# Gate product on VectorE from PSUM, every second unit's spectral products on GpSimd: a recurrence with a long convolution on one Trainium2 core

## Chip, cores and metric

The kernel runs on one core of a Trainium2 chip. The metric is device time in microseconds for one launch, the median over runs. The five instruction queues named below are TensorE (PE, with its weight loads as PEld), VectorE (DVE), ScalarE (ACT), GpSimd (POOL) and SyncE (SP, which issues the DMAs).

## What is computed

For each of 4 batches of 6272 steps and 256 channels, all float32 at the interface:

```python
sig = 1 / (1 + exp(-f_logit))
f = lower_bound + (1 - lower_bound) * sig
for t in range(6272):                       # a gated recurrence, per channel
    h = f[:, t] * h + (1 - f[:, t]) * x[:, t]
    y[:, t] = h
x1, x2, x3 = split(y @ w_proj, 3)           # 256 channels each
conv = irfft(rfft(x2) * rfft(filter_fft))   # circular, 6272 long, per channel
out = (x1 * conv * x3) @ w_out
```

## The kernel before

**Numbers of the transform.** 6272 is 128 times 49, so the long transform is two short ones written as matrix products: one over 128 points, one over 49. Channels are taken in pairs, 128 pairs in all, and handled in 16 *units* of 8 pairs.

**Stages of one batch.**
- *Recurrence* (`hgrn`): 13 pieces of 512 steps. `x` and `f_logit` are loaded, ScalarE makes the sigmoid (`sig`, L392), GpSimd multiplies it into x (`u`, L394, tile `XT`), TensorE transposes both (`sT`, `uT`, L401), ScalarE or VectorE makes the gate (`f`, L415), VectorE scans (`scan`, L423) into the f16 tile `HA`. GpSimd copies a part of the result behind its end (`wrap`, L371).
- *P*: the projection for x2, 98 matmuls (L730), copied out by ScalarE or VectorE (`x2`, into `X2`).
- *Spectrum*, per unit: first transform (`F1`, L743), its copy `A`, second transform (`F2`, L788) into two PSUM banks; two products with the filter's spectrum (`prod`, L801, on VectorE, 98 partitions by 1008) into tile `PP`; a small sum for frequency zero (`slot`, L793, on GpSimd), then the first inverse transform (`I2`, L811), and its copy `Th`. Every fourth unit has a `mini` product for frequency zero (L759, L765). The filter's spectrum was made in the setup, lies in DRAM and is fetched unit by unit into `Hu`. `PP` has two buffers (`NP = 2`), so even units use buffer 0 and odd units buffer 1; `Hu` has three.
- *Gate* (`gate`): in 13 column pieces of 490 and for two channel halves, 26 pieces a batch, two matmul pairs make x1 and x3 (`x13`, L450, one PSUM bank each); ScalarE copies both to SBUF (`xs`, L462, tiles `x1s` and `x3s`, two buffers); GpSimd multiplies them and writes the product regrouped from steps to the transform's order, f16, into `zt` (`z`, L466).
- *Output* (`phase_o`), 13 groups: the second inverse (`I1`, L844), VectorE multiplies it with `zt` (`y`, L850), TensorE applies w_out (L862), ScalarE or VectorE copies out (`o`, L363 on ScalarE), SyncE stores. The first `y` needs every `z` and, through I1, every `Th` of its batch; `zt` has one buffer, so the next batch's `z` follow this batch's last `y`.

A setup of about 88 us makes the transform tables and the filter's spectrum, beside batch 0's recurrence.

**What sets the order.** Nothing is issued as written. Each piece of work is an `op` with a guessed cost on each engine that may run it, and the class `Plan` simulates the engines and the 8 PSUM banks and picks the next op by earliest start, an urgency (longest way to the end, plus tables `LEAD` and `TILT` by kind and batch) and a shyness by kind and engine (`SHY`). Ops with several engines in their cost (the PSUM copies, `f`, `wrap`) go to the one it picks. It then emits every engine's queue in that order. PSUM is one tile of 8 banks, a matmul op takes one or two of them (`take`) and the last op that reads them frees them. So a change of one op's engine, cost or weight can move the whole order, the setup's too. The lines of the gate before:

```python
op("xs", {"ACT": 0.05 + n / 1200.0}, ...)          # for x1 and for x3
op("z", {"POOL": 0.1 + 3.68 * n / 1000}, ...,
   r=[("x1s", j, 0), ("x1s", j, 1), "cv"], w=[("z", jb, c)])
```

Of the kernel before, what the change touches and what calls it, by code (L numbers as in the profile page):

```python
# [9 lines left out]
F32 = mybir.dt.float32  # L10
# [3 lines left out]
AOP = mybir.AluOpType  # L14
AF = mybir.ActivationFunctionType
# [9 lines left out]
Q = 49  # L25
TB = 98
CH = 512
# [13 lines left out]
ZS = 64.0  # L41
# [16 lines left out]
class Plan:  # L58
# [11 lines left out]
    FROM = {"PE": 0.0, "ACT": 0.0, "DVE": 0.8, "POOL": 0.8, "SP": 0.75}  # L70
    TURN = 0.097
    COLD = 7.5
    SHY = {("A", "ACT"): 27, ("A", "DVE"): 27, ("Th", "ACT"): -10, ("Th", "DVE"): 779,
            ("afs", "ACT"): 51, ("afs", "DVE"): -12, ("f", "ACT"): -4, ("f", "DVE"): 452,
            ("f2", "ACT"): 100, ("f2", "DVE"): 126, ("fr", "ACT"): 290, ("fr", "DVE"): 2705,
            ("fr", "POOL"): -84, ("hw", "ACT"): -32, ("hw", "DVE"): 364, ("o", "ACT"): 13,
            ("o", "DVE"): 1968, ("wrap", "ACT"): 1376, ("wrap", "POOL"): 115, ("x2", "ACT"): 90,
            ("x2", "DVE"): 63}

    STICK = 4.0  # L80
    ROWS = ("F2", "mini", "I1", "FF2", "last")
    LANES = 8

    TILT = {
        "A": (10, -421, 208, -185), "F1": (-87, -1, 1, -163), "F2": (297, -97, -22, -362),
        "FF1": (-72, 0, 0, 0), "FF2": (-79, 0, 0, 0), "H": (-184, 334, 22, 133),
        "I1": (-280, -65, -92, 13), "I2": (-282, -43, -206, 0), "P": (-10, -2, 64, -49),
        "Th": (-3, -372, 21, -100), "afs": (-31, 0, 0, 0), "f": (-348, -382, -7, -601),
        "f2": (206, 0, 0, 0), "ff": (-455, 0, 0, 0), "fr": (-21, 0, 0, 0), "hst": (-91, 0, 0, 0),
        "hw": (11, 0, 0, 0), "load": (-7, -238, -192, 0), "mX": (18, 0, 0, 0),  # L90
        "mini": (-412, 357, -19, 94), "o": (0, -19, 214, 0), "pad": (14, 0, 0, 0),
        "prod": (0, -199, -22, 1135), "proj": (387, -1338, -11, 254), "rot": (-287, 0, 0, 0),
        "sT": (-25, 1516, -37, 149), "scan": (-40, -6, -71, -138), "sig": (-116, 262, -46, -451),
        "slot": (-6, -10, -78, 18), "store": (-23, -498, 174, 242), "tabs": (335, 0, 0, 0),
        "u": (-6, 0, -48, 383), "uT": (-1369, -27, 23, 104), "warm": (-427, 0, 0, 0),
        "wrap": (0, 312, 253, 2), "x13": (-140, -373, -471, -159), "x2": (35, -288, 339, 160),
        "xs": (2160, 1264, 0, 301), "y": (-27, 470, 49, -42), "z": (0, 0, 532, 756),
        "zm": (1130, 0, -12, 65),
    }

    LEAD = {
        "A": (35, -373, 1648, 137), "F1": (462, -629, 1502, 4000), "F2": (5639, 140, 319, 1412),
        "FF2": (-1269, 0, 0, 0), "H": (0, -477, -796, -1751), "I1": (-67, 978, 15, 184),
        "I2": (-35, -8, 4207, 55), "P": (-34, -342, 3292, -57), "Th": (164, 540, 125, 0),
        "args": (598, 0, 0, 0), "f": (294, -69, -69, -264), "f2": (-491, 0, 0, 0),
        "ff": (5684, 0, 0, 0), "fr": (505, 0, 0, 0), "hst": (566, 0, 0, 0), "hw": (-475, 0, 0, 0),
        "iden": (346, 0, 0, 0), "iota": (33, 0, 0, 0), "last": (43, 0, 0, 0),
        "load": (1910, -587, 70, -424), "mX": (103, 0, 0, 0), "mini": (162, -443, 3560, 2034),
        "o": (182, 252, -11, 418), "pad": (-134, 0, 0, 0), "pre": (-656, 0, 0, 0),
        "prod": (53, -700, 0, 7), "proj": (-7749, -9436, -6234, 114), "rest": (109, 0, 0, 0),  # L110
        "sT": (0, -96, -2, -1), "scan": (-892, 17, -1191, -2973), "sig": (0, 79, 43, 146),
        "slot": (126, 219, 502, 1379), "store": (-387, -299, -79, -369), "tabs": (5294, 0, 0, 0),
        "turns": (-46, 0, 0, 0), "u": (801, 3, 107, 648), "uT": (10, -692, -6798, -121),
        "warm": (-40, 0, 0, 0), "wcol": (443, 0, 0, 0), "wl": (-474, 0, 0, 0),
        "wrap": (-936, -549, -39, 333), "x13": (-350, -2412, -46, -1943), "x2": (0, 0, 1048, 2601),
        "xs": (5528, -104, 106, -88), "y": (-100, -570, -30, -285), "z": (-742, -2, 69, 0),
        "zm": (236, 148, 847, -6),
    }

    def __init__(self):  # L120
# [157 lines left out]
def kernel(  # L278
# [10 lines left out]
    nc = tc.nc  # L289
# [4 lines left out]
    op = plan.op  # L294

    konst = ctx.enter_context(tc.tile_pool(name="konst", bufs=1))
    iden = konst.tile([128, 128], F32, name="iden")
# [9 lines left out]
    W13 = konst.tile([128, 2, 512], F16, name="W13")  # L307
# [19 lines left out]
    Hu = konst.tile([128, NH, 2, 2, UE * 64], F16, name="Hu")  # L327
# [45 lines left out]
    def either(n, runs=1.0):  # L373

        return {"ACT": 0.045 + runs * n / 1200.0, "DVE": 0.07 + n / 960.0}
# [61 lines left out]
    def gate(b):  # L437
        for c in range(NCHK):
            m0 = c * XR
            nm = min(XR, 128 - m0)  # L440
            hn = [("hn", kh, i) for kh in range(2) for i in range(max(c - 1, 0), c + 1)]
            t0, n = m0 * Q, nm * Q
            for jb in range(2):
                x13 = []
                for i in range(2):
                    js = slice(i * 256 + jb * 128, i * 256 + jb * 128 + 128)

                    def mm(e, p, js=js, t0=t0, n=n):
                        for kh in range(2):
                            nc.tensor.matmul(PS[:, p, 0:n], W13[:, kh, js],  # L450
                                             HA[:, HB[kh] + t0:HB[kh] + t0 + n],
                                             start=(kh == 0), stop=(kh == 1))
                    x13.append(op("x13", {"PE": 0.005 + 2 * n / 2400.0}, mm,
                                  r=hn + ["W13"], w=["qX"], take=1))
                j = count["s"] % 2
                count["s"] += 1

                def xs(i, j=j, n=n):
                    return late["x3s" if i else "x1s"][:, j, 0:n]
                for i in range(2):  # L460
                    op("xs", {"ACT": 0.05 + n / 1200.0}, lambda e, p, xs=xs, n=n, i=i:
                       nc.scalar.activation(  # L462
                           xs(i), PS[:, p, 0:n], AF.Copy, scale=1.0 if i else ZS),
                       r=["cv"], w=[("x1s", j, i)], src=x13[i])
                op("z", {"POOL": 0.1 + 3.68 * n / 1000}, lambda e, xs=xs, jb=jb, m0=m0, nm=nm:
                   nc.gpsimd.tensor_tensor(  # L466
                       late["zt"][:, jb, :, m0:m0 + nm],
                       xs(0).rearrange("p (m r) -> p r m", r=Q),
                       xs(1).rearrange("p (m r) -> p r m", r=Q), op=AOP.mult),
                   r=[("x1s", j, 0), ("x1s", j, 1), "cv"], w=[("z", jb, c)])  # L470


    def prepare(tmp):
# [300 lines left out]
    def unit(b, u):  # L774
# [7 lines left out]
        def mm(e, xb):  # L782
# [11 lines left out]
            PP[:TB, k, :, :, :, 0], zp[:TB, u // NA % 2, :, :, 0, ka:ka + UE],  # L794
            zp[:TB, u // NA % 2, :, :, 1, ka:ka + UE], op=AOP.add),
           r=[("zp", u // NA % 2), "D1"], w=[("Pz", k, 0), ("Pz", k, 1)])
        for o in range(2):
            def prod(e, xb, o=o):
                px = PS[:TB, xb + o, :].rearrange("p (i k) -> p i k", k=64)[:, :, 1:64]
                hh = Hu[:TB, h, :, o].rearrange("p a (i k) -> p a i k", k=64)  # L800
                nc.vector.tensor_tensor(  # L801
                    PP[:TB, k, o, :, :, 1:64],
                    px.unsqueeze(1).broadcast_to([TB, 2, UE, 63]), hh[:, :, :, 1:64],
                    op=AOP.mult)
            op("prod", {"DVE": 1.11}, prod, r=[("Hu", h)], w=[("P", k, o)], src=f2, part=o)

        def inv(e, ib):
            for o in range(2):
# [68 lines left out]
    with tc.manual_schedule():  # L877
        scope = ctx.enter_context(ExitStack())
        prepare(scope.enter_context(tc.tile_pool(name="tmp", bufs=1)))
        hgrn(0)  # L880

        def turn(e):

            scope.close()
            cv = ctx.enter_context(tc.tile_pool(name="cv", bufs=1))

            late["zt"] = cv.tile([128, 2, Q, 128], F16, name="zt")
            late["Th"] = cv.tile([128, TB, 2, 64], F16, name="Th")
            late["ys"] = cv.tile([128, 2, 2, 512], F32R, name="ys")
            late["x1s"] = cv.tile([128, 2, CH], F32, name="x1s")  # L890
            late["x3s"] = cv.tile([128, 2, CH], F32, name="x3s")
            late["osb"] = [cv.tile([128, 4, 256], F32, name=f"osb{i}") for i in range(NO)]
        op("pre", {"SP": 0.01}, turn, r=FF1 + FF2, w=["cv"])

        for b in range(B):
            plan.batch = b
            spectrum(b)
            gate(b)
            phase_o(b)
            if b + 1 < B:  # L900
                plan.batch = b + 1
                hgrn(b + 1)
        plan.emit()
# [30 lines left out]
```

## Time and profile before

| | |
|---|---|
| median of 11 runs | 507.8 us (505.46 to 510.57) |
| the profiled execution | 508.18 us, its span 506.4 us |
| granted TensorE clock, mean | 0.994 |
| instructions | 13245 |
| DMA traffic | 116.39 MB, mean 230 GB/s |

The span runs from the first to the last instruction of the program on the chip; the time has 1.8 us more around it. Times in the profile are microseconds unless marked ns. A group of instructions reads: line, engine, operation, out<-in by the program's tile names, shapes, count, then busy time, mean ns of one, and the engine's idle time just before, with what ended it. The busy time of TensorE has modelled ends, since its matmuls are pipelined.

### The profile page before, as it was taken

To read this page: it belongs to the slowest core of one execution; us is meant where nothing else is said; L and a number is where in the kernel's file an instruction comes from. 1 tells how busy PE (TensorE), PEld (TensorE's weight loads), DVE (VectorE), ACT (ScalarE), POOL (GpSimd) and SP (SyncE) were. 2 spreads that over 40 slices of the span, in tenths; PEclk is the share of its full clock that TensorE was granted. 3 is DMA by queue.
4 is the path that set the end of the run, shared out by engine and by line. 5 is a ranking of instruction groups with operands and counts; after the bars stand their busy time and mean duration, and the time that the engine had idled before them with its cause. 6 is when DMAs were issued, how large, how long until landed. Compare 5 with 4: busy or idle time off the path is not lost. (4 is left out here: it accounts for less than half of the span.)

```text
span 506.4 us, 13245 instructions
## 1 busy us (share of the span) xinstructions
PE 479.4 (95%) x5257; PEld 373.9 (74%) x5257; DVE 444.0 (88%) x451; ACT 410.8 (81%) x587; POOL 386.5 (76%) x328
## 2 busy tenths in 40 slices
PE   8979998999999999998998999999999999999795
PEld 6767775866777899766766889666778887566584
DVE  8789996888999999888996999899999978989763
ACT  3658868999998787898898788899988767999554
POOL 8886765899999845599799848889989633998700
PEclk9999999999999999999999999999999999999999
DMA  8979999536678998256668997166798870345156
GB/s 333 408 231 291 322 299 300 193 109 187 211 217 270 299 354 305 97 180 172 206 208 282 294 328 318 42 191 179 245 297 287 308 287 12 97 132 158 34 237 273
DMA packets 41725, 116.39 MB, mean 230 GB/s; under 512 B 4384, under 2 KB 6304, under 8 KB 41664
## 3 DMA queue, kind: packets, MB, share of 16 engines
q1 hardware_dynamic: 41664, 115.56, 68.1%
q8 instruction: 41, 0.67, 0.6%
q14 instruction: 20, 0.16, 0.1%
HBM read 84.54 MB, written 31.00 MB: 228 GB/s over the span
## 5 line engine op out<-in xcount | busy, mean ns | idle before, releaser
L466 POOL TENSOR_TENSOR zt<-x1s,x3s 128x490 f16<-128x490 f32 (+1 forms) x104 | 201.5, 1953 | 39.7 <-ACT x3s L462 19.3
L801 DVE TENSOR_TENSOR PP<-PS,Hu 98x1008 f16<-98x1008 f32 x128 | 146.7, 1198 | 11.4 <-ACT x1s L462 3.9
L394 POOL TENSOR_TENSOR XT<-XT,FL 128x1024 f32<-128x1024 f32 (+1 forms) x52 | 117.2, 2257 | 36.8 <-DMA XT<-in_x_dram 18.2
L423 DVE TENSOR_TENSOR_SCAN HA<-fTs,HA,PS 128x512 f16<-128x512 f32 (+1 forms) x96 | 113.9, 1203 | 10.6 <-PE PS L401 7.4
L450 PE MATMUL PS<-HA,W 128*128 128x490 f16 (+1 forms) x416 | 106.3, 367 | 1.5 <-DVE PP L801 1.0
L415 ACT ACTIVATE fTs<-PS,nomc 128x512 f32<-128x512 f32 (+1 forms) x104 | 69.4, 669 | 20.3 <-PE PS L401 13.1
L850 DVE TENSOR_TENSOR ys<-PS,zt 128x1024 fp32r<-128x1024 f32 (+1 forms) x52 | 59.9, 1159 | 15.0 <-PE PS L844 8.3
L363 ACT ACTIVATE osb<-PS 128x1024 f32<-128x1024 f32 (+1 forms) x52 | 50.7, 978 | 22.0 <-PE PS L862 19.9
L401 PE MATMUL PS<-iden,XT 128*128 128x128 f32 x392 | 62.5, 280 | 3.7 <-ACT fTs L415 1.6
L462 ACT ACTIVATE x1s<-PS 128x490 f32<-128x490 f32 (+1 forms) x104 | 60.9, 585 | 5.7 <-PE PS L450 3.7
L862 PE MATMUL PS<-Wo,ys 128*128 128x256 f32 x392 | 60.3, 296 | 3.5 <-DVE ys L850 2.0
L462 ACT ACTIVATE x3s<-PS 128x490 f32<-128x490 f32 (+1 forms) x104 | 60.6, 584 | 3.3 <-POOL zt L466 2.1
L401 PE MATMUL PS<-iden,FL 128*128 128x128 f32 x392 | 60.6, 275 | 0.3 <-ACT FL L392 0.3
L392 ACT ACTIVATE FL<-FL 128x1024 f32<-128x1024 f32 (+1 forms) x52 | 52.6, 1015 | 7.8 <-DMA FL<-in_f_logit_dram 7.7
L811 PEld LDWEIGHTS <-PP 98*128 98x128 f16 x1024 | 50.1, 98 | 10.8 <-issue 2.6
L862 PEld LDWEIGHTS PS<-Wo,ys 128*128 128x128 f32 x392 | 50.5, 192 | 8.0 <-DVE ys L850 2.7
L361 ACT CAST Th<-PS 128x784 f16<-128x784 f32 x64 | 52.7, 824 | 4.2 <-PE PS L811 3.7
L401 PEld LDWEIGHTS PS<-iden,XT 128*128 128x128 f32 x392 | 44.1, 140 | 16.1 <-POOL XT L394 2.6
L450 PEld LDWEIGHTS <-W 128*128 128x128 f16 x416 | 34.7, 97 | 27.0 <-issue 8.7
L811 PE MATMUL PS<-VA,PP 98*128 98x98 f16 x512 | 52.4, 207 | 1.5 <-DVE PP L801 0.7
L811 PE MATMUL PS<-VB,PP 98*128 98x98 f16 x512 | 52.1, 207 | 0.0
L366 DVE CAST X<-PS 128x1024 f16<-128x1024 f32 (+1 forms) x34 | 46.9, 1481 | 5.2 <-PE PS L730 3.9
(98 smaller groups left out, 700.4 us busy)
## 6 DMA issues: line engine op xcount, KB each, us to landing
Hu<-H SPq DMA_DIRECT2D x64, 392.0 KB
FL<-in_f_logit_dram SPq DMA_DIRECT2D x48, 512.0 KB
XT<-in_x_dram SPq DMA_DIRECT2D x48, 512.0 KB
out_dram<-osb SPq DMA_DIRECT2D x48, 512.0 KB
X<-in_moe_filter_fft_dram SPq DMA_DIRECT2D x9, 512.0 KB
H<-Hu SPq DMA_DIRECT2D x16, 196.0 KB
H<-Hu SPq DMA_DIRECT2D x16, 128.0 KB
Hu<-in_moe_filter_fft_dram SPq DMA_DIRECT2D x2, 512.0 KB
```

The lines of the kernel that those rows point to most:

```text
L361: nc.scalar.copy(dst, src)
L394: op("u", {"POOL": 0.1 + 0.553 * nb}, lambda e, xt=xt, ft=ft: nc.gpsimd.tensor_tensor(xt, xt, ft, op=AOP.mult), r=[("ft", k)], w=[("xt", k)])
L401: nc.tensor.transpose(PS[:, p, j:128 * nb:nb], src[:, j, cols], iden[:])
L415: nc.scalar.activation(fT, PS[:, p, 0:n], AF.Identity, scale=by, bias=1.0)
L423: nc.vector.tensor_tensor_scan(h, fT, PS[:, p, 0:n], init, op0=AOP.mult, op1=AOP.add),
L450: nc.tensor.matmul(PS[:, p, 0:n], W13[:, kh, js], HA[:, HB[kh] + t0:HB[kh] + t0 + n], start=(kh == 0), stop=(kh == 1))
L462: nc.scalar.activation(xs(i), PS[:, p, 0:n], AF.Copy, scale=1.0 if i else ZS),
L466: nc.gpsimd.tensor_tensor(late["zt"][:, jb, :, m0:m0 + nm], xs(0).rearrange("p (m r) -> p r m", r=Q), xs(1).rearrange("p (m r) -> p r m", ...
L801: nc.vector.tensor_tensor(PP[:TB, k, o, :, :, 1:64], px.unsqueeze(1).broadcast_to([TB, 2, UE, 63]), hh[:, :, :, 1:64], op=AOP.mult)
L811: nc.tensor.matmul(PS[:, ib + o, pr * TB:(pr + 1) * TB], PP[:TB, k, o, n, 2 * pr:2 * pr + 2, :], v[:TB], start=(n == 0), stop=(n == 1))
L850: nc.vector.tensor_tensor(late["ys"][:, yk, :, 0:rn * 128], PS[:, cb:cb + 2, 0:rn * 128], late["zt"][:].rearrange("p k r m -> p k (r m)") ...
L862: nc.tensor.matmul(po[:, i, :], late["ys"][:, yk, kh, i * 128:(i + 1) * 128], Wo[:, kh, :], start=(kh == 0), stop=(kh == 1))
```

## The change

The copy of x1 to SBUF goes. x3 is made first and copied by ScalarE with the scale that x1 had; VectorE then multiplies x1, straight from its PSUM bank, with it, and writes `zt`. For odd units the two banks of F2 are copied to a new SBUF tile `Xc` (one buffer, in the space of `x1s`) by ScalarE or VectorE, and GpSimd makes both products from it (`prodp`). Even units keep theirs on VectorE. The tables `SHY`, `TILT` and `LEAD` have other values throughout; the new kinds `xc` and `prodp` are in them. Costs of all other ops, buffer counts and the matmuls are as they were.

```diff
     SHY = {("A", "ACT"): 31, ("A", "DVE"): 44, ...,
+           ("xc", "ACT"): 24, ("xc", "DVE"): 452}
 ...
-                x13 = []
-                for i in range(2):
+                x13 = {}
+                for i in (1, 0):
 ...
-                for i in range(2):
-                    op("xs", {"ACT": 0.05 + n / 1200.0}, lambda e, p, xs=xs, n=n, i=i:
-                       nc.scalar.activation(
-                           xs(i), PS[:, p, 0:n], AF.Copy, scale=1.0 if i else ZS),
-                       r=["cv"], w=[("x1s", j, i)], src=x13[i])
-                op("z", {"POOL": 0.1 + 3.68 * n / 1000}, lambda e, xs=xs, jb=jb, m0=m0, nm=nm:
-                   nc.gpsimd.tensor_tensor(
+                op("xs", {"ACT": 0.05 + n / 1200.0}, lambda e, p, j=j, n=n: nc.scalar.activation(
+                    late["x3s"][:, j, 0:n], PS[:, p, 0:n], AF.Copy, scale=ZS),
+                   r=["cv"], w=[("x3s", j)], src=x13[1])
+                op("z", {"DVE": 0.1 + n / 930.0}, lambda e, p, j=j, n=n, jb=jb, m0=m0, nm=nm:
+                   nc.vector.tensor_tensor(
                        late["zt"][:, jb, :, m0:m0 + nm],
-                       xs(0).rearrange("p (m r) -> p r m", r=Q),
-                       xs(1).rearrange("p (m r) -> p r m", r=Q), op=AOP.mult),
-                   r=[("x1s", j, 0), ("x1s", j, 1), "cv"], w=[("z", jb, c)])
+                       PS[:, p, 0:n].rearrange("p (m r) -> p r m", r=Q),
+                       late["x3s"][:, j, 0:n].rearrange("p (m r) -> p r m", r=Q), op=AOP.mult),
+                   r=[("x3s", j), "cv"], w=[("z", jb, c)], src=x13[0])
 ...
+        beside = u % 2 == 1
+        if beside:
+            op("xc", either(1024), lambda e, xb: copy(e, late["Xc"][:TB], PS[:TB, xb:xb + 2, :]),
+               r=["cv"], w=["Xc"], src=f2)
         for o in range(2):
-            def prod(e, xb, o=o):
-                px = PS[:TB, xb + o, :].rearrange(...)[:, :, 1:64]
+            def prod(e, xb=None, o=o):
+                px = (late["Xc"][:TB, o] if beside else PS[:TB, xb + o, :]).rearrange(...)[:, :, 1:64]
                 hh = Hu[:TB, h, :, o].rearrange("p a (i k) -> p a i k", k=64)
-                nc.vector.tensor_tensor(
+                (nc.gpsimd if beside else nc.vector).tensor_tensor(
                     PP[:TB, k, o, :, :, 1:64],
                     px.unsqueeze(1).broadcast_to([TB, 2, UE, 63]), hh[:, :, :, 1:64],
                     op=AOP.mult)
-            op("prod", {"DVE": 1.11}, prod, r=[("Hu", h)], w=[("P", k, o)], src=f2, part=o)
+            if beside:
+                op("prodp", {"POOL": 2.4}, prod, r=[("Hu", h), "Xc"], w=[("P", k, o)])
+            else:
+                op("prod", {"DVE": 1.11}, prod, r=[("Hu", h)], w=[("P", k, o)], src=f2, part=o)
 ...
-            late["x1s"] = cv.tile([128, 2, CH], F32, name="x1s")
+            late["Xc"] = cv.tile([128, 2, 512], F32, name="Xc")
```

## Prediction

> **What bounds the kernel now.** I read the page first: five engines close together.
>
> ```profile
> PE 479.4 (95%) x5257; PEld 373.9 (74%) x5257; DVE 444.0 (88%) x451; ACT 410.8 (81%) x587; POOL 386.5 (76%) x328
> ```
>
> TensorE is busiest, but a whole-span share hides stages, so I cut the span by stage (a batch's spectrum, then its inverse and output with the next recurrence). Columns: stretch, length, busy time (instructions) of PE, PEld, DVE, ACT, POOL, clock, DMA share, GB/s.
>
> ```profile
> 104.40:160.00 55.60, 54.81 (x647) 39.29 (x647) 52.62 (x53) 53.03 (x86) 53.55 (x41) 1.00 0.66 209
> 210.00:265.00 55.00, 52.77 (x627) 36.78 (x623) 51.65 (x52) 48.60 (x79) 49.56 (x41) 1.00 0.60 182
> 317.20:366.90 49.70, 49.42 (x600) 34.61 (x599) 46.14 (x47) 46.62 (x74) 45.89 (x38) 1.00 0.55 166
> 423.50:466.00 42.50, 41.82 (x513) 27.37 (x512) 38.16 (x38) 38.82 (x62) 37.53 (x30) 1.00 0.36 108
> 466.00:479.80 13.80, 10.80 (x158) 7.00 (x156) 10.47 (x12) 9.39 (x17) 11.60 (x10) 1.00 0.23 61
> ```
>
> In the spectrum stages VectorE, ScalarE and GpSimd all run at 88 to 96% beside a full TensorE; none is spare. The durations come from the groups by line:
>
> ```profile
> L466 POOL TENSOR_TENSOR zt<-x1s,x3s 128x490 f16<-128x490 f32 x96 | 188.8, 1982 | 39.0 <-ACT x3s L462 19.3 <-DVE ys L850 12.6 <-DMA XT<-in_x_dram 4.1
> L801 DVE TENSOR_TENSOR PP<-PS,Hu 98x1008 f16<-98x1008 f32 x128 | 146.7, 1198 | 11.4 <-ACT x1s L462 3.9 <-ACT x3s L462 3.3 <-ACT Th L361 1.8
> L394 POOL TENSOR_TENSOR XT<-XT,FL 128x1024 f32<-128x1024 f32 x48 | 114.3, 2383 | 35.5 <-DMA XT<-in_x_dram 16.9 <-ACT FL L392 11.0 <-ACT fTs L415 7.4
> L466 POOL TENSOR_TENSOR zt<-x1s,x3s 128x392 f16<-128x392 f32 x8 | 12.8, 1610 | 0.7 <-ACT x1s L462 0.7
> L394 POOL TENSOR_TENSOR XT<-XT,FL 128x256 f32<-128x256 f32 x4 | 2.9, 736 | 1.3 <-DMA XT<-in_x_dram 1.3
> L850 DVE TENSOR_TENSOR ys<-PS,zt 128x1024 fp32r<-128x1024 f32 x48 | 58.1, 1217 | 14.9 <-PE PS L844 8.3 <-POOL zt L466 3.3 <-ACT osb L363 1.8
> L850 DVE TENSOR_TENSOR ys<-PS,zt 128x256 fp32r<-128x256 f32 x4 | 1.9, 464 | 0.1
> ```
>
> Last, the chain that ended last, at the turn from spectrum to output of batch 3 (start, length, what):
>
> ```profile
> 466.85 1.55 POOL zt L466
> 468.77 0.55 POOL PP L793 x2
> 469.32 0.98 POOL zt L466
> 470.30 0.79 issue
> 471.45 1.81 POOL zt L466
> 473.56 3.36 POOL zt L466 x2
> 476.92 1.54 POOLq L929
> 478.48 1.24 DVE ys L850
> ```
>
> The last z ends at 478.4 and the first y starts. But the timeline has that batch's last spectral inverse (L811) ending at 476.4 and its first output inverse (L844) at 477.3: z and spectrum finish together, so removing z there buys at most 1 us. In batches 1 and 2 L811 ends at 266.9 and 375.1 and y starts at 276.4 and 383.4, each right after the last z (276.0, 383.4): 9.5 and 8.3 us, against 2.9 and 2.1 in batches 0 and 3. TensorE filled that time with the next batch's transposes (17.18 of 17.8 us from 366.9 to 384.7), so most of it isn't lost.
>
> **TensorE's floor.** Pieces of the same chain view: F1 8 matmuls 0.45 to 0.55 us, F2 0.54, I2 0.70, four gate matmuls 0.83, four transposes 0.44, 16 of L844 0.56, 8 of L862 0.95, and 98 of L730 in 10.8. Per batch: 16x(0.5+0.54+0.70) + 26x0.83 + 98x0.22 + 12.25x(0.56+0.95) + 10.8 = 100 us. The batches' L730 starts (88.5, 193.7, 306.2, 413.7) are 105, 112.5 and 107.5 apart; the last batch takes 87.4 against 78 without transposes. So some 34 us at most is there to win.
>
> **The change part by part.**
> *VectorE.* It loses 64 of 128 products: 64x1.198 = 76.7 us. It gains 104 z from PSUM. By y's two sizes, (1217-464)/768 = 0.98 ns an element over 0.21 us: 0.69 for 490, 0.60 for 392, in all 71 us. z reads at a stride of 49 and writes runs of 10 f16. The filter's copy reads PSUM as far apart at 692 ns for 512 (against 677 for a plain 512), so a strided read needn't cost; the X copies that write runs of four f16 take 1501 for 1024, 1.47 ns, which makes z 0.93 and the sum 96. I take 0.69, as the runs are longer: -5 us net, +20 at worst; below nothing is excluded, since both operands are f32.
> *ScalarE.* It loses 104 x1 copies, 60.9 us, and gains 32 copies of 1024 from PSUM, 1.02 us each by the A copy (46.9/46): 33 us. Net -28. On VectorE each would be 1.21.
> *GpSimd.* It loses all z, 201.5 us. It gains 64 products of 1008. Near end: the x-times-gate product has packed operands, (2383-736)/768 = 2.14 ns, so 2.35 us. Far end: z's slope (1982-1610)/98 = 3.8 ns, 3.95 us; low end a one-input f32 copy, 1.05 us for 1024. The new operands are packed in runs of 63, so I take 2.35: 150 us, net -51. That GpSimd is slowed by VectorE's work beside it does not show: the gate products took 2.35 to 2.47 us whichever VectorE rows ran at the time.
> GPSIMD Engine Reference in the Trainium skill (Performance pitfalls) says reads with a step over 8 bytes cost half as much again; the two slopes, 3.8 at a 196-byte step against 2.14, agree in sign and show more. By the page's ratio a packed product would be 3.8/1.5 = 2.5 ns an element, 2.7 us (an estimate), and my sum 6 us higher. Against the change, the same page (Engine selection) tells one to keep two-input elementwise work on VectorE, GpSimd being about twice as slow; it gives 4497 ns for 2048, by which (an estimate) a product is 2.21 us and my sum 2 us lower (16 products of batch 3's chain).
>
> *Where that sits.* All three feeders get lighter, VectorE and ScalarE by 33 us together. The flexible copies (A, X, filter) can be spread over both, and over batches 0 to 2 the two spare 25 us, 12.6 each, 13.7 of time at 92% occupancy if they set the pace throughout. TensorE's floor takes part back: I count two thirds, -9. Of the 6 us each that y waited for z in batches 1 and 2, a quarter, -3, as TensorE was filled.
>
> *What is added to a chain.* Product tile PP has two buffers by unit parity and the new Xc one, so GpSimd's next unit starts only after I2 read the last product, and after the copy that waits for the last product to leave Xc. A pair of units costs GpSimd 2x2.35 for products, 0.4 for two slot sums (0.2 from start to start by the timeline), and idle time: a hand-over (0.08, from x3's copy at 466.77 to z), 1.02 of copy, another, perhaps 0.3 behind other work on a 91% busy ScalarE, less the even slot: 1.2 (I2's way is shorter: 0.34 from a product's end to its weights at 470.6, 0.70, a hand-over). So 6.3 us a pair, 50 for eight. Before, batches ran their units (L801 to L811) in 59.8, 56.4, 52.2 and 45.4 us. In 0 to 2 that fits; in batch 3 it doesn't: F2 at 430.2, first copy done near 432, last product near 481.5, output inverse near 483.5 instead of 477.3. +6 us, where TensorE has nothing else.
>
> *Other waits.* z now stands in VectorE's queue, waiting for the x3 copy (0.59 us); behind it stand products, scans and y, and I2 waits for those. x1's PSUM bank stays until z is done, about 1 us longer 104 times, while 32 F2 pairs come free after 1.0 us of copy instead of 2.3 us of products: 104 against 83 bank-us, nothing net; if banks were the limit, 20/8 = 3 us. The filter tile Hu (3 buffers) of odd units is held for 4.7 us instead of 2.4; SyncE waits 150 us for such releases already, with loads and stores queued behind; three buffers span 9 us of units, so nothing, or 2 us a batch if a load of the next recurrence is late. The new weights of the order also touch the setup (0 to 88.5 us): 0, +-3.
>
> Sum against the profiled execution's own time: 508.2 - 9 - 3 + 6 = 502.2. That execution is 0.4 above the median, so 502.
>
> **Rivals.**
> *Slower: GpSimd's product chain sets the spectrum stage in every batch.* The recurrence's products (2.38 each) share that in-order queue: 6, 3 and 3 ran inside the unit stages of batches 0 to 2. Behind 51 us of chain these become 65, 58 and 58 against 59.8, 56.4 and 52.2: +5, +2, +6, and batch 3 +6; the loads taken off the other engines then buy only the wait for z, -3 to -6. About 523 if none is moved, 514 if four are. For: one buffer, one in-order queue, the longest operations between F2 and I2. Against: GpSimd had holes outside these stages (it was busy 16.26 of 29.1 us from 384.7 on) where they fit. It decides early: each 0.1 us on a product is 1.6 us a batch, 6.4 in all; from about 2.45 us a piece my gain is gone.
> *Nothing much:* TensorE's 95% is real, relief goes into idle time, z's stride costs VectorE what the products saved: 507 to 508.
> *Everything is won:* batches 0 to 2 keep 6 of their 25 us above the floor, batch 3 stays level: 488.
> *z not really freed:* z's strided form costs 0.93 on VectorE: 104x0.24 = 25 us more, half of it shed to ScalarE, 502 + 12 = 514. I count it with the slower rival.
>
> **How the numbers follow.** Forecast (494 to 507) 0.53, slower rivals 0.31, nothing much 0.09, everything won 0.07. The range, 489 to 518, leaves out the best part of "everything won" and the slower rival with nearly nothing moved, about a tenth each. About 0.3%, 1.5 us, is what a measurement can tell from no change. Faster: the forecast but for 0.03, and the best case, 0.57. Same: those 0.03 and most of "nothing much", 0.10. Slower: 0.33.
>
> **What would show it.** Right: VectorE near 438, ScalarE 383 (or both levelled near 410), GpSimd near 335; z on VectorE near 0.69; products on GpSimd near 2.35; first y within 3 us of the last I2 in batches 1 and 2; unit stage of batch 3 near 51 us. Wrong: products over 2.5, GpSimd idle over 1.5 us a pair for Xc or I2, or unit stages of 60 us and more.

## The result, and the profile after

The change makes the kernel a little slower, clear of noise: 513.92 us median (511.64 to 516.04) against 506.72 for the kernel before in the runs beside it, a ratio of 1.0134 with a 95% interval of 1.0109 to 1.0160. The forecast was 502; the rival "z not really freed" had 514. The profiled execution has a span of 512.5 us. Ratios here and below leave out executions in a slower state, which the medians include, so the two can differ a little.

The busy times of the changed kernel, from its page:

```profile
PE 483.4 (94%) x5257; PEld 377.8 (74%) x5257; DVE 451.9 (88%) x483; ACT 403.1 (79%) x524; POOL 320.3 (62%) x287
```

Against the kernel before, GpSimd lost 66 us and ScalarE 8, as work was taken from both; VectorE gained 8 instead of losing 5. The groups by line of the changed kernel tell why (line, engine, operation, shapes, count, busy us, mean ns, idle before):

```profile
L463 DVE TENSOR_TENSOR zt<-PS,x3s 128x490 f16<-128x490 f32 x96 | 94.6, 1012 | 5.3 <-PE PS L452 4.3 <-ACT x3s L459 0.9
L802 POOL TENSOR_TENSOR PP<-Xc,Hu 98x1008 f16<-98x1008 f32 x64 | 134.6, 2114 | 60.6 <-ACT Xc L363 55.4 <-PE PS L815 3.3 <-DMA Hu<-H 1.2
L802 DVE TENSOR_TENSOR PP<-PS,Hu 98x1008 f16<-98x1008 f32 x64 | 75.7, 1203 | 7.5 <-PE PS L785 6.3 <-ACT Th L363 0.6 <-ACT HA L363 0.6
L363 ACT COPY Xc<-PS 98x1024 f32<-98x1024 f32 x32 | 32.5, 1016 | 1.2 <-PE PS L785 1.2
```

One z takes 1.01 us on VectorE, not 0.69 and not even the 0.93 of the far end: 100.8 us in all (with the shorter ones) where the sum had 71. GpSimd's product is cheaper than assumed, 2.11 against 2.35, and the copy to `Xc` is as priced, 1.02.

The changed kernel by stretches: the unit stages of its four batches (first product to last I2), and the turn after the third. Columns as in the prediction: stretch, length, busy time (instructions) of PE, PEld, DVE, ACT, POOL, clock, DMA share, GB/s.

```profile
104.60:174.20 69.60, 67.74 (x757) 49.93 (x757) 69.12 (x71) 60.79 (x87) 59.00 (x43) 1.00 0.76 232
202.20:282.10 79.90, 78.12 (x888) 58.51 (x885) 72.74 (x74) 69.49 (x97) 59.33 (x46) 1.00 0.82 249
309.50:395.70 86.20, 83.87 (x950) 63.22 (x947) 79.09 (x81) 71.84 (x99) 59.50 (x44) 1.00 0.76 245
395.70:407.40 11.70, 10.77 (x138) 8.78 (x136) 11.66 (x13) 6.70 (x10) 5.85 (x11) 1.00 0.24 92
423.20:483.60 60.40, 58.41 (x736) 40.66 (x731) 50.83 (x57) 49.10 (x66) 37.89 (x32) 1.00 0.46 152
```

VectorE is busy for 99% of the first stage and all of the turn, and for 91, 92 and 84% of the other stages, beside a TensorE at 97 to 98%; GpSimd, once as full as the others, is at 63 to 85% in the unit stages. The end of the chain that ended last, in batch 3 (start, length, what):

```profile
477.96 0.85 PE PS L815 x16
478.81 3.74 PE PS L452 x18
482.56 1.02 DVE zt L463
483.66 0.50 ACT x3s L459
484.16 0.36 ACT Th L363
484.51 0.32 issue
484.84 0.51 ACT x3s L459
485.37 0.83 DVE zt L463
486.29 1.24 DVE ys L854
```

z is still what the first y waits for, now on VectorE. Eight z run back to back from 477.8 to 485.2. In that time ScalarE's copies of x3 wait four times for z to free their buffer (0.33 to 0.68 us each). The gate's matmuls (L452) ahead of the last I2 in TensorE's queue don't wait: 18 take 3.74 us, the pace at which four took 0.83 us in the kernel before.

### The profile page after: what moved, and what is told of

It is laid out like the page before. It is cut to its first block, busy times and chain, and to the rows that moved or that the text cites. A ratio compares the mean times of both kernels' runs of the same rounds, so it can differ in the third digit from the quotient of the medians.

```text
span 512.5 us, 13213 instructions
## 1 busy us (share of the span) xinstructions
PE 483.4 (94%) x5257; PEld 377.8 (74%) x5257; DVE 451.9 (88%) x483; ACT 403.1 (79%) x524; POOL 320.3 (62%) x287
## 5 line engine op out<-in xcount | busy, mean ns | idle before, releaser
L802 POOL TENSOR_TENSOR PP<-Xc,Hu 98x1008 f16<-98x1008 f32 x64 | 134.6, 2114 | 60.6 <-ACT Xc L363 55.4
L452 PE MATMUL PS<-HA,W 128*128 128x490 f16 (+1 forms) x416 | 105.0, 367 | 1.3 <-DVE HA L425 0.8
L463 DVE TENSOR_TENSOR zt<-PS,x3s 128x490 f16<-128x490 f32 (+1 forms) x104 | 100.8, 999 | 5.5 <-PE PS L452 4.3
L417 ACT ACTIVATE fTs<-PS,nomc 128x512 f32<-128x512 f32 (+1 forms) x101 | 67.7, 670 | 27.9 <-PE PS L403 18.0
L802 DVE TENSOR_TENSOR PP<-PS,Hu 98x1008 f16<-98x1008 f32 x64 | 75.7, 1203 | 7.5 <-PE PS L785 6.3
L452 PEld LDWEIGHTS <-W 128*128 128x128 f16 x416 | 36.7, 98 | 27.4 <-issue 7.9
L363 ACT CAST HA<-PS 128x1024 f16<-128x1024 f32 x52 | 51.6, 1019 | 4.4 <-PE PS L740 4.0
L790 POOL TENSOR_TENSOR PP<-zp 98x32 f16<-98x32 f16 x64 | 20.3, 342 | 55.0 <-PE PS L815 42.1
```

The lines of the kernel that those rows point to most:

```text
L363: nc.scalar.copy(dst, src)
L417: nc.scalar.activation(fT, PS[:, p, 0:n], AF.Identity, scale=by, bias=1.0)
L452: nc.tensor.matmul(PS[:, p, 0:n], W13[:, kh, js], HA[:, HB[kh] + t0:HB[kh] + t0 + n], start=(kh == 0), stop=(kh == 1))
L463: nc.vector.tensor_tensor(late["zt"][:, jb, :, m0:m0 + nm], PS[:, p, 0:n].rearrange("p (m r) -> p r m", r=Q), late["x3s"][:, j, 0:n].rearr ...
L802: (nc.gpsimd if beside else nc.vector).tensor_tensor(PP[:TB, k, o, :, :, 1:64], px.unsqueeze(1).broadcast_to([TB, 2, UE, 63]), hh[:, :, :, ...
```

## The experiments

Three theories stand against each other. Theory Z: z's price, 30 us of VectorE above the sum, costs the time. Theory C, the slower rival of the prediction: the chain on GpSimd of the copy, two products and I2 sets the unit stages. Theory O: the order that the plan made costs the time. Kernels marked *same order* keep every queue as in the changed kernel, since the plan's costs and dependences are untouched, so only durations differ (the halved products add one zeroing in the setup). The setup is everything up to the first matmul of batch 0's projection P, L727 in the changed kernel. It took between 84.6 and 93.5 us in the profiled executions, so beside the time I give the part of the span from there on: 417.9 us before, 424.7 for the changed kernel.

**e1, z without regrouping** (same order).

```diff
-                       late["zt"][:, jb, :, m0:m0 + nm],
-                       PS[:, p, 0:n].rearrange("p (m r) -> p r m", r=Q),
-                       late["x3s"][:, j, 0:n].rearrange("p (m r) -> p r m", r=Q), op=AOP.mult),
+                       late["zt"][:, jb].rearrange("p r m -> p (r m)")[:, m0 * Q:(m0 + nm) * Q],
+                       PS[:, p, 0:n], late["x3s"][:, j, 0:n], op=AOP.mult),
```

> The changed kernel with z's regrouping left out: z reads x1 and x3 and writes zt straight, so its output is not the reference's; every queue's order is the same. Theory Z (z was mis-sized: 1.01 us against 0.69, 33 us of VectorE): z falls to about 0.69 us, VectorE from 452 to about 419 us, and the time comes back by 8 to 13 us, to 501 to 506. Theory C (the chain on GpSimd of Xc's copy, two products and I2, 7 us a pair of units, sets the unit stages): 0 to -3 us, 511 or more.

498.46 us, below the 501 to 506 expected for Z, ratio 0.9824 (0.9767 to 0.9881); z 0.658 us, VectorE 420.8 us; 409.3 us from there on. Z holds: the access patterns of one instruction are worth 15 us.

**e2b, half of GpSimd's products left out** (same order).

```diff
+  n = UE // 2 if beside else UE
-      PP[:TB, k, o, :, :, 1:64], px..., hh[:, :, :, 1:64]
+      PP[:TB, k, o, :, 0:n, 1:64], px[:, 0:n]..., hh[:, :, 0:n, 1:64]
```

> The changed kernel with GpSimd's products made for 4 of the 8 channel pairs of an odd unit (the other half of the tile is zeroed once in the setup, so the output is not the reference's); same order. A product takes about 1.1 us instead of 2.1. Theory C (GpSimd's chain sets the unit stages): the pair period in the last batch falls from 7.0 to about 5 us and the time by 10 to 20 us, to 494 to 504. Theory Z (z's 1.01 us on VectorE): VectorE has as much to do as in the changed kernel, 0 to -4 us, 510 or more. After the straight z gave 498 and the regrouped x3 501, Z expects the latter.

514.33 us, ratio 1.0168 (1.0130 to 1.0206); 424.9 us from there on, 0.2 more than the changed kernel. The timeline of GpSimd in batch 3 of the changed kernel:

```profile
442.52 4.18 POOL L802 TENSOR_TENSOR PP<-Xc,Hu 98x1008 f16<-98x1008 f32 x2
446.66 0.34 POOL L790 TENSOR_TENSOR PP<-zp 98x32 f16<-98x32 f16 x1
449.09 0.34 POOL L790 TENSOR_TENSOR PP<-zp 98x32 f16<-98x32 f16 x1 [2.09 <-PE PS L815]
449.50 4.19 POOL L802 TENSOR_TENSOR PP<-Xc,Hu 98x1008 f16<-98x1008 f32 x2
```

and the same place with half the product:

```profile
442.06 2.26 POOL L804 TENSOR_TENSOR PP<-Xc,Hu 98x504 f16<-98x504 f32 x2
444.28 0.34 POOL L791 TENSOR_TENSOR PP<-zp 98x32 f16<-98x32 f16 x1
448.64 0.34 POOL L791 TENSOR_TENSOR PP<-zp 98x32 f16<-98x32 f16 x1 [4.01 <-PE PS L817]
449.05 2.26 POOL L804 TENSOR_TENSOR PP<-Xc,Hu 98x504 f16<-98x504 f32 x2
```

The products take 1.9 us less and GpSimd waits 1.9 us more for I2; the period stays at 7.0, and batch 3's unit stage at 60.3 us. GpSimd keeps up with the others and does not set their pace. Theory C falls.

**e7, the forms one by one**, four of each behind the end of the kernel before.

> The kernel before with 48 products and copies of one gate piece behind its end (their results go nowhere), four of each form, to price the operands one by one; the added tail is 40 to 60 us. VectorE, 490 elements: all as in the change about 1.01 us; x1 strided from PSUM alone 0.66; x3 strided from SBUF alone 1.01 if that is the cost; runs of ten in the output alone 0.66; all straight 0.66. GpSimd: as before 1.95; packed inputs with runs of ten 1.1 to 1.3 by the gate product's 2.14 ns an element; all straight the same. ScalarE: straight, strided read and strided write all near 0.59, as the regrouped copy gave 0.588.

The groups by line of that tail, one line a form:

```profile
L918 DVE TENSOR_TENSOR zt<-PS,x3s 128x490 f16<-128x490 f32 x4 | 3.9, 975 | 2.3 <-ACT osb L363 2.2
L920 DVE TENSOR_TENSOR zt<-PS,x3s 128x490 f16<-128x490 f32 x4 | 2.7, 669 | 0.1
L922 DVE TENSOR_TENSOR zt<-PS,x3s 128x490 f16<-128x490 f32 x4 | 3.9, 972 | 0.1
L924 DVE TENSOR_TENSOR zt<-PS,x3s 128x490 f16<-128x490 f32 x4 | 2.7, 666 | 0.1
L928 DVE TENSOR_TENSOR zt<-PS,x3s 128x490 f16<-128x490 f32 x4 | 2.7, 666 | 0.1
L930 POOL TENSOR_TENSOR zt<-x1s,x3s 128x490 f16<-128x490 f32 x4 | 7.6, 1906 | 40.3 <-DVE zt L926 40.1
L932 POOL TENSOR_TENSOR zt<-x1s,x3s 128x490 f16<-128x490 f32 x4 | 4.9, 1215 | 0.3
L936 ACT ACTIVATE x3s<-PS 128x490 f32<-128x490 f32 x4 | 2.3, 579 | 34.5 <-POOL zt L934 34.4
L938 ACT ACTIVATE x3s<-PS 128x490 f32<-128x490 f32 x4 | 2.3, 579 | 0.1
L940 ACT ACTIVATE x3s<-PS 128x490 f32<-128x490 f32 x4 | 4.0, 992 | 0.1
```

On VectorE: z as changed 975 ns (L918); only x1 strided, from PSUM, 669 (L920); only x3 strided, from SBUF, 972 (L922); only the output in runs of ten 666 (L924); all straight 666 (L928). The whole price is the SBUF read at a stride of 49 f32. GpSimd: 1906 as before (L930), 1215 with packed inputs (L932). ScalarE: straight 579 (L936), strided PSUM read 579 (L938), strided SBUF write 992 (L940), where the expectation had all three near 590. So the regrouping is free where it is a read from PSUM. This is one execution, with four of each form.

**e8 and e15, x3 regrouped by its copy** (same order; the kernel computes all of the result).

```diff
-  late["x3s"][:, j, 0:n], PS[:, p, 0:n], AF.Copy, scale=ZS)
+  late["x3s"][:, j, 0:n].rearrange("p (r m) -> p r m", r=Q),
+  PS[:, p, 0:n].rearrange("p (m r) -> p r m", r=Q), AF.Copy, scale=ZS)
 ...
-  late["x3s"][:, j, 0:n].rearrange("p (m r) -> p r m", r=Q), op=AOP.mult)
+  late["x3s"][:, j, 0:n].rearrange("p (r m) -> p r m", r=Q), op=AOP.mult)
```

> The changed kernel, same order, but ScalarE's copy of x3 does the regrouping of x3, so that VectorE's z reads x3 packed and only x1 at a stride (from PSUM); the output is the reference's. If z's 1.01 us comes from the strided SBUF read, z falls to about 0.69 and, by theory Z, the time to 501 to 508, provided ScalarE's copy stays near 0.59 us; if ScalarE's copy rises to 0.8, 22 us of ScalarE are added and half of the gain is lost. If z's price comes from the strided PSUM read or the runs of ten in its output, z stays near 1.0. Theory C: 512 to 514 either way.

> The regrouped x3 again, over five rounds beside the run above, since its first ratio to the kernel before reached up to 0.997: expected 500 to 502 and a ratio of 0.985 to 0.993. A ratio that takes in 1 would mean that the packed read only brings the change back to where it started.

e8: 500.79 us, ratio 0.9895 (0.9822 to 0.9968). e15, the same kernel: 499.36 us, 0.9874 (0.9832 to 0.9916). Both times lie just under the expected ranges, by 0.2 and 0.6 us. From the end of the setup on 410.5 and 409.1 us. The groups by line of e8 show z cheaper and the copy at its old price:

```profile
L464 DVE TENSOR_TENSOR zt<-PS,x3s 128x490 f16<-128x490 f32 x96 | 62.0, 658 | 11.8 <-PE PS L452 7.1 <-ACT x3s L459 4.0 <-issue 0.2
L459 ACT ACTIVATE x3s<-PS 128x490 f32<-128x490 f32 x96 | 56.1, 588 | 7.8 <-PE PS L452 6.6 <-DVE zt L464 0.5
```

This version is faster than the kernel before by a little over 1%, and than the changed one: with the strided read moved to a place where it is free, the change lands in the forecast's 494 to 507. Its unit stages, for the last part of this document:

```profile
105.20:171.50 66.30, 66.09 (x758) 49.53 (x753) 63.54 (x72) 61.30 (x89) 58.47 (x43) 1.00 0.79 244
198.90:276.70 77.80, 76.52 (x888) 58.56 (x885) 66.02 (x75) 68.68 (x96) 58.31 (x45) 1.00 0.82 252
303.30:385.90 82.60, 81.78 (x950) 63.00 (x946) 72.33 (x81) 71.56 (x100) 57.91 (x43) 1.00 0.79 254
412.40:470.80 58.40, 57.81 (x735) 40.55 (x730) 44.52 (x57) 49.43 (x67) 37.85 (x32) 1.00 0.48 157
```

**e13, the regrouping for half of the pieces** (same order): e8's edit for one of the two channel halves.

> The changed kernel, same order, with x3 regrouped by ScalarE for one of the two channel halves only, so 52 of the 104 z read x3 packed (0.66 us) and 52 at a stride (1.01). Theory Z, as a dose: half of the 13 us of the full regrouping, 505.5 to 509. If the gain came from a few places where z is last in a chain, it could be anywhere from 500 to 514, and the batches would not share it evenly.

504.55 us, ratio 0.9955 (0.9913 to 0.9996), a little below the expected 505.5; VectorE 436.0 us, 415.9 us from the end of the setup on. Half the dose gives 8.8 of 14.2 to 15.6 us, and every batch gains, 1.8 to 2.8 us from one batch's first L727 to the next: no single place.

**e14, the same time taken off VectorE elsewhere** (same order): e2b's edit for the even units' products, on VectorE, instead.

> The changed kernel, same order, z as in the change (1.01 us), but VectorE's own products, those of the even units, made for 4 of 8 channel pairs (the other half of the tile zeroed once; output not the reference's): 64 products fall from 1.20 to about 0.69 us, 33 us of VectorE, as much as the packed z saves. If what counts is VectorE's load, wherever it is taken off: 498 to 505, VectorE near 420. If z's own length counts (it holds a PSUM bank, the x3 buffer and I2's place behind x13): 509 to 514.

509.49 us, ratio 1.0032 (1.0008 to 1.0056), the upper case by the time. But the zeroing that the experiment adds stands ahead of the copies of tables that lie in the same tile: VectorE waited 4.39 us for it, and the setup ended at 93.5, 5.7 us later than in the changed kernel. From there on it took 414.1 us, 10.6 less than the changed kernel, with 27.1 us less on VectorE (424.8). So time taken off VectorE elsewhere is worth nearly as much as at z: 0.39 us for each us here, 0.46 to 0.50 at z, 0.55 in e13. That speaks for VectorE's load as most of z's price, but it isn't parted cleanly: the shorter products also free F2's banks and start I2 sooner, and z may have a share by its own length (its bank, the x3 buffer). The figures are too close to show it.

**e12, half of GpSimd's products with the regrouped x3** (same order).

> The kernel with regrouped x3 (501 us), same order, and GpSimd's products made for 4 of 8 channel pairs (the other half of the tile zeroed once; output not the reference's). With z at 1.01 us the halved product brought nothing. If GpSimd's chain is the next bound once z is cheap, 490 to 497 and pair periods of the last batch below 6 us; if it is still hidden, 499 to 502 and periods as they were (6.0 to 7.1).

503.10 us, 1 us above the upper range of the expectation, ratio 0.9916 (0.9884 to 0.9949); 411.5 us from the end of the setup on, no gain over e8's 410.5, and batch 3's unit stage takes 58.4 us in both. GpSimd's chain is hidden there too.

**e9, the regrouping in the kernel before** (its own order): both copies regroup, GpSimd's z reads packed inputs.

> The kernel before, same order, with ScalarE's copies of x1 and x3 doing the regrouping, so that GpSimd's z reads both packed. If a strided read from SBUF is what is dear on GpSimd too, z falls from 1.98 to 1.1 to 1.3 us and GpSimd from 386 to about 310 us. z and the units end together in the kernel before, and y waited for z by 6 us in two batches where TensorE was filled: 502 to 507. If GpSimd had set the time, 490 to 500.

505.67 us, ratio 0.9989 (0.9959 to 1.0018). Its page:

```profile
PE 479.2 (95%) x5257; PEld 374.2 (74%) x5257; DVE 444.2 (88%) x451; ACT 409.8 (81%) x587; POOL 313.9 (62%) x328
```

73 us less on GpSimd, z at 1.23 instead of 1.98, and no time gained: before the change GpSimd looked as full as the others in the unit stages, but did not set their pace.

**e3, z on VectorE and all products there too** (`beside = False`).

> Only the first part of the change: z on VectorE from PSUM, all 128 products on VectorE as before, no copy Xc; the plan orders it anew with the changed tables. VectorE then has 452 + 77 = 529 us of work. Both theories expect it slower than the changed kernel, at 545 to 580, bound by VectorE; if it comes under 530, VectorE's load is not what sets the time.

569.34 us, ratio 1.1218 (1.1144 to 1.1292), in the range; VectorE has 510.2 us of work, 90% of the span. The plan made another order for this kernel, so its 55 us above the changed kernel are not shown to be VectorE's load alone.

**e11, e5 and e10: the order.** e11: the changed kernel planned with measured costs. e5: the kernel before with the changed tables. e10: e8 with measured costs.

```diff
-  op("z", {"DVE": 0.1 + n / 930.0}, ...          op("prodp", {"POOL": 2.4}, ...
+  op("z", {"DVE": 0.1 + 1.78 * n / 1000.0}, ...  op("prodp", {"POOL": 2.07}, ...   # e11
+  op("z", {"DVE": 0.09 + 1.06 * n / 1000.0}, ... op("prodp", {"POOL": 2.07}, ...   # e10
```

> The changed kernel with the measured costs in the plan (z 0.1 + 1.78 ns an element, GpSimd's product 2.07 us) instead of 0.63 and 2.4, so the order is another. Theory O (the order was made for wrong costs, and that is what costs the time): back to 500 to 508. Theory Z (the work itself, 33 us more on VectorE): 510 to 522, as the weights fit the old costs.

> The kernel before, its work unchanged, ordered with the changed tables SHY, TILT and LEAD (the kinds xc and prodp don't occur in it). It prices the order alone: if the tables hardly matter, 504 to 510; if weights made for other work and costs give a worse order, 515 to 540, as the changed kernel with corrected costs gave 532.

> The kernel with regrouped x3, planned with the measured costs (z 0.09 + 1.06 ns an element, GpSimd's product 2.07 us), tables as in the change; the plan makes another order. z's cost hardly moves (0.61 for 0.63), GpSimd's product does (2.07 for 2.4). Theory O: a plan nearer to the truth, 495 to 500. If the tables only fit the costs that they were made with: 505 to 530.

In this order: 531.71 us (ratio 1.0489, 1.0443 to 1.0534); 581.49 us (1.1454, 1.1411 to 1.1497); 505.18 us (0.9922, 0.9895 to 0.9949). e11 and e10 miss the ranges expected for O as the cause, and e11 and e5 lie above both of their ranges. Truer costs gave no better order: 18 us worse for the changed kernel, and no clear difference for e8, whose interval overlaps e10's. Tables made for one kernel cost the other 74 us. So another order can cost more than the change itself, and these tables fit best the costs that they came with; whether new tables for z at its true price would lower the 514 wasn't tried.

## Why the prediction was wrong

**The step that failed is z's price on VectorE.** The sum took 0.69 us, from y's two sizes, and argued from the filter's copy that a strided read costs nothing, with 20 us at worst. The copy's strided operand lies in PSUM; z has one in PSUM and one in SBUF. e7 parts the two: 669 ns and 972 ns. No VectorE row of the kernel before reads SBUF f32 at a stride, but one of GpSimd does, z itself: 3.8 ns an element against 2.14 for packed operands. The prediction used that row as a property of GpSimd. For VectorE, the Trainium skill, Vector Engine (DVE) Microarchitecture Reference (Measured stream behaviour on trn2), lists one source that hops 4 KiB at every element at 1.73 ns a column against 1.05 with all contiguous. This case's rows agree at a hop of 196 bytes: by the two sizes of z, (1012 - 838)/98 = 1.78 ns an element and, packed in e8, (658 - 555)/98 = 1.05. That row spoke against the change, and the sum didn't weigh it.

**What the failed term is worth.** 30 us of VectorE: e1, e8 and e15 take it away and win 14.2 to 15.6 us of span. Without it the change gains 7.4 to 8.8 us over the kernel before from the end of the setup on; the sum had -6. The total is near, its parts are not. From one batch's first L727 to the next (the last to the end) the kernel before took 105.2, 112.5, 107.4 and 92.7 us, e8 94.6, 104.4, 109.2 and 102.4. The first two stretches win more than the sum had, the third nothing, and the last loses 9.7 where the sum had 6, for another reason (below). Work moved between the stretches with the order, so it is in part luck that the total agrees.

**VectorE and ScalarE.** The sum had the two 33 us lighter together. In e8 they are, 822.8 us against 854.8 before; in the changed kernel, at 855.0, z's excess takes all of it. ScalarE took copies over (52 of A instead of 46, 23 of X instead of 18) and went from 411 to 403, but z's excess stayed on VectorE, which went to 452.

**The chain on GpSimd.** Forecast +6 us in batch 3 and the main slower rival. The rows fit it at first sight: unit stages of 69.6, 79.8, 86.2 and 60.3 us, pairs some 7.0 us apart in batch 3 against the forecast 6.3, GpSimd idle over 2 us a pair. e2b and e12 show that the products do not make it so; so no run shows the sum's +6 for this chain. e8, faster than the kernel before, has stages of 66.3, 77.7, 82.6 and 58.4 as well: the new order puts more other work among the units (in the changed kernel batch 2's output matmuls run until 443.3, 20 us into batch 3's units; before, they ended at 426.7, ahead of batch 3's first product at 431.0). The sign that the prediction named for "wrong", unit stages of 60 us and more, says nothing about the time.

**The rival that came true**, "z not really freed", had the instruction, its engine and the number 514. The number is in part luck. Its 0.93 us came from copies that write short runs, while e7 shows that the output costs nothing and the read of x3 everything, at 1.01. And it had half of the excess shed to ScalarE, while none was: e1 and e8, with a cheap z, give ScalarE the same copies. What came out near a half is another thing: each us of the excess on VectorE cost 0.46 to 0.50 us of time. The rival was counted in with the chain instead of being given the weight that the far end, left open by the trace, called for.

**Right beside these:** the copy at 1.02 us, GpSimd's product nearer to the packed row than to z's (2.11), and y following I2 by 4.2 and 3.0 us in batches 1 and 2 instead of 9.5 and 8.3.

## What to carry to other kernels

Price each operand of an instruction by itself: its memory, its step, its run length. When a trace has the operand's access pattern only on another engine, take that row as a warning for this engine too. Where these forms occur, let the instruction that reads from PSUM do the regrouping, and keep what goes through SBUF packed. An engine that is full beside others need not set their pace: making its work lighter at an unchanged order tells it in one run.

## What the hardware showed that was not expected

- VectorE reads SBUF f32 at a stride of 196 bytes at 1.78 ns an element against 1.05 packed (changed kernel and e8); the same stride from PSUM costs next to nothing (669 against 666 ns for 490, e7), and f16 output runs of ten cost nothing (666).
- ScalarE's copy of 490 f32: a strided PSUM read is free (579 ns, as straight), a strided SBUF write is not (992, e7).
- GpSimd: 1906 ns for 490 elements with both f32 inputs strided, 1215 packed (e7), and 2.11 us for 1008 elements on 98 partitions with one f32 and one f16 input, a little less an element than the 2.38 us for 1024 on 128 partitions with f32 throughout.
